# A fused attention and token-mixing kernel: a new order of all steps on every engine, other piece widths for the first filler products, and one store moved

## The chip, the cores and the metric

The kernel runs on one core of one Trainium2 chip. The metric is the time of one execution on the device, in microseconds (us); lower is better. A core has five engines that each work through a queue of their own in order: TensorE (PE: matrix products, with a second stream for its weight loads, PEld), VectorE (DVE), ScalarE (ACT), GpSimd (POOL) and SyncE (SP, which here only issues DMAs). Engines wait for one another by semaphores. Loads that change the type from f32 to bf16 are issued by POOL; plain stores and loads by SP, ACT or POOL.

## The reference

Two stages over 8 batches. Attention has 8 heads of 64 columns and 576 rows; the packed queries `p` have 32 rows.

```python
p_packed = sm_attn(p, k, v)            # softmax(p k^T / 8) v          (32 x 64 per head)
out      = sm_attn(q, p_packed, p_packed)   # softmax(q p_packed^T / 8) p_packed
x  = out as (batch, 576, 512)
wq, wk = x @ w_q, x @ w_k              # 512 -> 64
W_tok  = einsum('bsd,btd->bst', wq, wk) / 8
mixed  = einsum('bst,btd->bsd', W_tok, x)
result = relu(mixed) @ w_out           # 8 x 576 x 512, f32
```

## The kernel before, in words

Everything is unrolled, batch by batch, and written as steps. One string, `ORDER`, lists all 522 steps; the loop at its end (lines 604 to 625) runs through it and issues each step's instructions. The order of the string is therefore the order within each engine's queue: two steps on different engines may overlap, two on the same engine may not pass each other. A step is written `NAME.batch.part@engine=banks`: `@A` is ACT, `@V` DVE, `@P` POOL; a step without a letter is PE's, except loads (`LD`, issued by POOL unless marked) and stores (`ST`, `STF`, `STH`, issued by SP unless marked). The number after `=` names the 2 KB PSUM banks that the product is written to.

The steps of one batch, with the line where the instruction is recorded (copies are recorded in helpers: L127 on ACT, L131 on DVE, L129 on POOL; block transposes in L242):

| step | engine | what | line |
|---|---|---|---|
| LD.k, LD.v, LD.q (LD.r, LD.g: half of one) | POOL | load with f32 to bf16; v is two DMAs | L179, L176, L185 (L182, L156) |
| LD.E, LD.H | ACT, SP | first p and half of k of batch 0, as f32 | L164, L171 |
| EC, HC, EX, PB | ACT, DVE | turn these into the operands of the first products | L127, L242, L131 |
| KT, QV, PT | DVE | block transpose of k, of q, of the packed result | L242 |
| S1, X1, TE | PE, ACT, DVE | p k^T; exponential; transpose of it | L278/L288, L296/L299, L242 |
| PV, RC, PP | PE, DVE, DVE | times v; reciprocal of the sum; scaling | L321, L325, L329 |
| QK, QKE, QD | PE, ACT or DVE, any | packed result times w_k, w_q; copy; second copy | L342, L127/L131/L129 |
| S2, X2, RS, RR, AM | PE, ACT, DVE, DVE, DVE or POOL | q times packed result; exponential; row sums; reciprocal; scaling | L379, L384, L400, L405, L411 |
| AT, AE | PE, copy | transpose; copy to SBUF | L425/L420 |
| WKQ, WE, GM, GE, Y, YE | PE and copies in turn | the two 64-column products, x^T wk, and its product with the packed result | L447/L452, L473, L483, L490/L492 |
| MX, MR, RL, RLR | PE, ACT or DVE | mixing product (MR: the rest rows) and relu | L498, L504, L509/L511 |
| OT, OE (OEF, OH, OEH) | PE, copy | tiles of relu times w_out, and copies of them; OT.b.4 is the rest rows of two batches | L546/L583 |
| ST (STF, STH) | SP, POOL, ACT | 512 KB (256, 128 KB) of the output | L565, L567, L592, L596 |

`WARM.n=bank` (lines 615 to 621) multiplies zeros: n x 128 columns of f32, in pieces of at most 512 columns, whose result nobody reads. Each f32 piece leaves two records in the trace. They fill PE's queue where nothing else is ready: 27 units ahead of the first real product S1.0, 12 steps with 78 units in all, the last just ahead of batch 3. `HOLD.v7` is a tiny DMA on SP that waits for the last load of v, so that SP's stores behind it don't begin earlier. `SET` steps write constants and zeros; `SET.tab` is a tiny exponential on ACT.

There are four buffers each for k, v and q, six for the output, two or three for most others. Eight loads may be under way on POOL's queue; the next one waits for the eighth before it.

Of the kernel before, what the change touches and what calls it, by code (L numbers as in the profile page):

```python
# [11 lines left out]
ORDER = """
SET.warm@V LD.E0@A LD.H@S LD.g0 SET.mask@V LD.E1@S LD.W0 SET.v0@V EC@A LD.v0 SET.tab@A HC@A LD.q0 LD.W1
SET.pz0@V EX@V PB.0.1@V PB.0.0@V SET.idf@V SET.aff@P PB.0.3@V PB.0.2@V KT.0.1@V KT.0.0@V QV.0.1@V WARM.27=0
S1.0=0,1,2 X1.0.0@A WARM.6=3 PV.0.0=4,5 PV.0.1 RC.0@V PP.0.0@V PP.0.1@V PT.0@V WARM.6=3 QK.0=3 LD.r0 QV.0.0@V
SET.v1@P SET.v3@P WARM.1=6 S2.0.2=6,7 LD.k1 S2.0.0=0,1 LD.P2 X2.0.0@A S2.0.1=4,5 RS.0.0@V LD.P3 X2.0.1@A
X2.0.2@A SET.v2@V RS.0.2@V RR.0.2@V AM.0.2@V KT.1.2@V RS.0.1@V RR.0.1@V LD.P0 RR.0.0@V AM.0.0@V LD.v1
WARM.18=2 S1.1=0,1,2 SET.idb@V AM.0.1@V QKE.0@A QD.0@V WARM.3=4 AT.0.2=3 SET.aT0@V X1.1.0@A AT.0.0=4 AE.0.0@A
PV.1.0=6,7 LD.P1 PX@V LD.q1 LD.k2 LD.v2 AE.0.2@A PV.1.1 RC.1@V PP.1.1@V SET.aT1@V AT.0.1=5 AE.0.1@V
WKQ.0.0=0,1 WARM.2=2 WKQ.0.1 WKQ.0.2 WE.0.0@A SET.aT2@V WE.0.1@A WARM.4=2 GM.0=7 GE.0@A WARM.1=2 Y.0=2,3  # L20
QV.1.2@V PP.1.0@V PT.1@V S2.1.1=4,5 KT.2.2@V LD.q2 X2.1.1@A S2.1.0=0,1 S2.1.2=6,7 YE.0@A MX.0.0=4,5 LD.k3 LD.O
LD.v3 X2.1.2@A S1.2=2,3,6,7 RS.1.1@V RR.1.1@V AM.1.1@P X2.1.0@A RS.1.0@V RR.1.0@V X1.2.1@A X1.2.0@A TE.2.1@V
WARM.5=0 AT.1.1=0 AE.1.1@A RL.0.0@A AM.1.0@P QK.1=1 TE.2.0@V QKE.1@A QD.1@A LD.k4 PV.2.0=6,7 PV.2.1 AT.1.0=2
RS.1.2@V RR.1.2@V AM.1.2@V AT.1.2=3 AE.1.2@A AE.1.0@V WARM.2=0 WKQ.1.0=4,5 LD.q3 WKQ.1.2 WKQ.1.1 WE.1.0@A
MR.0=0,1 MX.0.1=2,3 RC.2@V WE.1.1@A GM.1=4 RLR.0@A QV.2.2@V RL.0.1@A PP.2.0@V PP.2.1@V PT.2@V KT.3.2@V QK.2=5
QKE.2@A S2.2.3=6,7 S2.2.2=0,1 GE.1@A LD.v4 X2.2.3@A Y.1=2,3 YE.1@V X2.2.2@A WARM.3=5 MX.1.1=4,5 MR.1=6,7
# [11 lines left out]
LD.q7 S1.6=0,1,4,5 ST.0.0@P OE.2.0@A PT.5@V AE.4.3@V WKQ.4.0=6,7 QV.5.2@V WKQ.4.1 X1.6.1@A X1.6.0@A TE.6.0@V
WKQ.4.2 OT.3.0=2,3 OT.3.1 WE.4.2@A MR.3=4,5 RLR.3@A TE.6.1@V S2.5.2=0,1 S2.5.3=6,7 OE.3.0@V X2.5.3@A X2.5.2@A
HA.5@P GM.4=4 OT.3.4=5 OEF.3.4@A ST.2.1 GE.4@V Y.4=2,3 YE.4@A PV.6.0=6,7 PV.6.1 RC.6@V ST.1.4 QV.6.2@V  # L40
PP.6.1@V QK.5=4 QKE.5@A MX.4.0=0,1 ST.2.0 RL.4.0@A PP.6.0@V PT.6@V RS.5.4@V RR.5.4@V AM.5.3@P QD.5@A
MX.4.1=2,3 RL.4.1@A OT.3.2=4,5 KT.7.2@V OT.3.3 S2.6.2=0,1 X2.6.2@A OE.3.1@A S2.6.3=6,7 X2.6.3@A MR.4=2,3
RLR.4@V RS.6.4@V OT.4.0=0,1 OT.4.1 OE.4.0@A AM.5.2@P QK.6=4 S1.7=6,7,2,3 X1.7.1@A AT.5.3=5 OT.4.2=0,1 AT.5.2=2
QKE.6@A ST.3.1 X1.7.0@A AE.5.3@V WKQ.5.0=4,5 QD.6@V WKQ.5.1 AE.5.2@A WKQ.5.2 RR.6.4@V AM.6.3@V OT.4.3 TE.7.1@V
AT.6.3=3 TE.7.0@V AE.6.3@V AM.6.2@P WE.5.2@A GM.5=6 PV.7.0=4,5 PV.7.1 OE.4.1@A QV.7.0@V GE.5@A Y.5=0,1 RC.7@V
PP.7.1@V PP.7.0@V AT.6.2=7 WKQ.6.0=2,3 WKQ.6.1 QV.7.1@V AE.6.2@A WKQ.6.2 PT.7@V YE.5@A MR.5=6,7 MX.5.0=0,1
RL.5.0@V ST.1.0 RLR.5@A WE.6.2@A MX.5.1=4,5 OT.5.4=6 RL.5.1@A GM.6=7 GE.6@A S2.7.2=2,3 X2.7.2@A S2.7.1=0,1
S2.7.0=4,5 OEF.5.4@V RS.7.2@V QK.7=7 ST.0.1@P ST.4.1@P ST.3.4@P QKE.7@V Y.6=2,3 RR.7.2@V AM.7.2@P OT.5.0=6,7
X2.7.1@A ST.3.0 X2.7.0@A YE.6@A MX.6.1=0,1 RS.7.0@V MR.6=4,5 RLR.6@A RR.7.0@V AM.7.0@P RS.7.1@V MX.6.0=2,3
OT.5.1 RL.6.1@A OT.5.2=4,5 OE.5.0@A RR.7.1@V AM.7.1@V ST.5.4 AT.7.0=0 ST.1.1 AT.7.1=1 RL.6.0@A AT.7.2=6 ST.4.0  # L50
ST.5.0 QD.7@V OT.5.3 AE.7.2@A OE.5.1@A AE.7.0@V WKQ.7.0=2,3 WKQ.7.2 AE.7.1@V WKQ.7.1 OT.6.0=0,1 WE.7.0@V
WE.7.1@A GM.7=7 GE.7@A OT.6.1 ST.5.1 OE.6.0@V Y.7=4,5 YE.7@A OT.6.2=2,3 MX.7.0=6,7 MX.7.1=4,5 OEF.6.2@V
# [7 lines left out]
def kernel(  # L60
# [542 lines left out]

    with tc.manual_schedule():
        for item in ORDER.split():
            name, _, bk = item.partition("=")
            name, _, eng = name.partition("@")
            f = name.split(".")
            if f[0] == "LD":
                load(f[1], eng)  # L610
            elif f[0] in ("HOLD", "TOUCH"):
                hold(f[1])
            elif f[0] == "SET":
                setup(f[1], eng)
            elif f[0] == "WARM":
                n = 128 * int(f[1])
                while n > 0:
                    w = min(n, 512)
# [1 line left out]
                    nc.tensor.matmul(bank(int(bk), [w]), warm[:, 0:P], rhs, start=True, stop=True)  # L620
# [33 lines left out]
```

## Time and profile before

| | us |
|---|---|
| median of 3 runs | 106.24 (105.89 to 106.82) |
| the profiled execution | 105.26 |
| its span, first to last instruction | 103.5 |
| busy: PE / DVE / ACT / POOL | 93.6 / 76.4 / 65.9 / 47.3 |
| products on zeros (L620), busy | 21.4, all before 37.5 |
| OT products (L546), busy | 29.5 and 3.6 |
| first real product / last product ends | 9.57 / 99.0 |

The times of instructions come from the profiled execution, so that a sum over them is made against 105.26 us: 103.5 of span and 1.8 around it. The page has the busy tenths of each engine in 40 slices of 2.6 us, the chain of work that ended last, groups of instructions by line, and the DMA queues. The timeline gives start and duration of each instruction (or of neighbouring equal ones, with x and their number), and in brackets how long the engine was idle before it and what ended that. The tensor clock was granted at 1.0 throughout.

### The profile page before, as it was taken

To read this page: it belongs to the slowest core of one execution; us is meant where nothing else is said; L and a number is where in the kernel's file an instruction comes from. 1 tells how busy PE (TensorE), PEld (TensorE's weight loads), DVE (VectorE), ACT (ScalarE), POOL (GpSimd) and SP (SyncE) were. 2 spreads that over 40 slices of the span, in tenths; PEclk is the share of its full clock that TensorE was granted. 3 is DMA by queue.
4 is the path that set the end of the run, shared out by engine and by line. 5 is a ranking of instruction groups with operands and counts; after the bars stand their busy time and mean duration, and the time that the engine had idled before them with its cause. 6 is when DMAs were issued, how large, how long until landed. Compare 5 with 4: busy or idle time off the path is not lost.

```text
span 103.5 us, 3532 instructions
## 1 busy us (share of the span) xinstructions
PE 93.6 (90%) x1502; PEld 54.5 (53%) x1518; DVE 76.4 (74%) x152; ACT 65.9 (64%) x116; POOL 47.3 (46%) x67
## 2 busy tenths in 40 slices
PE   5997999999799899978999999999999899999920
...
DVE  5146265999898889598797979749999988549510
ACT  0190406063588986578999879889987798936220
...
PEclk9999999999999999999999999999999999999999
DMA  2999999999999999999999999999999999995794
GB/s 87 245 176 205 198 206 201 208 213 208 209 212 213 205 208 212 213 208 212 212 209 209 212 210 206 219 208 204 212 284 403 408 412 416 398 421 221 284 379 161
DMA packets 14015, 25.16 MB, mean 243 GB/s; under 512 B 2160, under 2 KB 7024, under 8 KB 14000
## 3 DMA queue, kind: packets, MB, share of 16 engines
...
q8 instruction: 12, 0.20, 0.7%
q10 hardware_dynamic: 416, 0.20, 0.7%
...
HBM read 30.28 MB, written 9.44 MB: 384 GB/s over the span
## 4 chain that ended last, share of the span: by engine, by line
PE 59%; DMA 15%; DVE 8%; ACT 6%; POOL 5%; issue 2%; SPq 0%; ACTq 0%; POOLq 0%; DVEq 0%
PE ps L546 23%; DMA k_sb<-in_k_dram 12%; PE ps L620 9%; PE ps L321 4%; PE ps L379 4%; POOL a L411 4%; DMA o<-in_p_dram 3%; PE ps L452 3%; PE ps L425 3%; DVE kT L242 3%; PE ps L278 2%; PE ps L473 2%; DVE rs L400 2%; PE ps L498 2%; PE ps L447 2%
## 5 line engine op out<-in xcount | busy, mean ns | idle before, releaser
L546 PE MATMUL ps<-wout,relu 128*128 128x512 bf16 x111 | 29.5, 380 | 1.4 <-ACT wkq L127 0.6
L620 PE MATMUL ps<-o 128*128 128x512 f32 (+3 forms) x50 | 21.4, 555 | 1.2 <-DVE o L134 1.2
L411 POOL TENSOR_TENSOR a<-e,rr 128x256 bf16<-128x256 f32 (+2 forms) x12 | 14.9, 1247 | 16.5 <-ACT e L384 8.7
L546 PEld LDWEIGHTS <-relu 128*128 128x128 bf16 x124 | 10.8, 98 | 12.6 <-issue 2.1
L127 ACT ACTIVATE o<-ps 128x1024 f32<-128x1024 f32 (+2 forms) x14 | 12.7, 917 | 3.6 <-DMA out_dram<-o 2.0
L384 ACT ACTIVATE e<-ps 128x256 f32<-128x256 f32 (+2 forms) x19 | 11.1, 629 | 5.5 <-PE ps L379 5.5
L620 PEld LDWEIGHTS ps<-o 128*128 128x128 f32 x50 | 9.2, 203 | 9.2 <-issue 7.2
L242 DVE STREAM_TRANSPOSE qT<-q_sb 128x1152 uint32<-128x1152 uint32 (+1 forms) x10 | 11.2, 1121 | 3.1 <-DMA q_sb<-in_q_dram 3.1
L400 DVE TENSOR_REDUCE rs<-e 128x16 f32<-128x512 f32 (+2 forms) x13 | 11.1, 855 | 3.1 <-ACT e L384 2.9
L509 ACT ACTIVATE relu<-ps 128x1024 bf16<-128x1024 f32 (+1 forms) x12 | 11.7, 988 | 0.7 <-PE ps L498 0.7
L176 POOL DMA_DIRECT2D v_sb<-in_v_dram x16 | 10.1, 632 | 4.4 <-DMA q_sb<-in_q_dram 1.7
L242 DVE STREAM_TRANSPOSE kT<-k_sb 128x1152 uint32<-128x1152 uint32 (+1 forms) x9 | 11.0, 1228 | 0.5 <-DMA k_sb<-in_k_dram 0.4
L127 ACT ACTIVATE wkq<-ps 128x448 bf16<-128x448 f32 (+1 forms) x10 | 7.1, 731 | 3.2 <-PE ps L447 2.1
L131 DVE COPY o<-ps 128x512 f32<-128x512 f32 (+2 forms) x6 | 4.9, 824 | 3.8 <-PE ps L546 1.7
L299 ACT ACTIVATE e1T<-ps 128x576 bf16<-128x576 f32 x12 | 7.4, 656 | 0.3 <-PE ps L288 0.2
L321 PE MATMUL ps<-v_sb,e 64*64 64x192 bf16 x288 | 7.5, 245 | 0.1
L179 POOL DMA_DIRECT2D k_sb<-in_k_dram x7 | 5.1, 730 | 5.0 <-DMA k_sb<-in_k_dram 3.2
L452 PE MATMUL ps<-aT,pqk 128*128 128x256 bf16 (+1 forms) x48 | 6.7, 247 | 0.3 <-POOL pqk L129 0.3
L321 PEld LDWEIGHTS <-e 64*64 64x64 bf16 x288 | 5.8, 107 | 1.8 <-DVE e L242 0.6
L296 ACT ACTIVATE e<-ps 128x1152 bf16<-128x1152 f32 x2 | 2.3, 1130 | 7.0 <-PE ps L278 7.0
L379 PE MATMUL ps<-ppT,qT 64*128 64x64 bf16 x320 | 6.3, 190 | 0.0
L185 POOL DMA_DIRECT2D q_sb<-in_q_dram x6 | 4.3, 723 | 4.2 <-DMA q_sb<-in_q_dram 2.5
...
## 6 DMA issues: line engine op xcount, KB each, us to landing
...
q_sb<-in_q_dram POOLq DMA_DIRECT2D x6, 576.0 KB, 13.8
...
```

What stands on the lines that cost most here:

```text
L127: nc.scalar.activation(o, i, COPY)
L176: nc.gpsimd.dma_start(v_bufs[b % NL][halves(i), 0:7:2], src)
L242: nc.vector.transpose(o, i)
L321: nc.tensor.matmul(T["pv", b][halves(cc), i], lhsT, rhs, start=n == 0, stop=n == R - 1, skip_group_check=True)
L379: nc.tensor.matmul(ps[:, y, t - t0, i], lhsT, rhs, start=e == 0, stop=e == 1)
L384: nc.scalar.activation(e2[:, t0:t1].rearrange("a t (i y n) -> a y (t i) n", i=2, y=2), T["s2", b, c].rearrange("a y t i n -> a y (t i) n") ...
L400: nc.vector.tensor_reduce(rs[:, t0 * H:t1 * H], src, axis=AX, op=ADD)
L411: e.tensor_tensor(a2[:, t0:t1].rearrange("a t i (u l) -> a (t i u) l", l=L), e2v(b, c), T["rr", b][:, t0 * H:t1 * H].to_broadcast((P, (t1 ...
L452: nc.tensor.matmul(o, pqk[:, i, Dl:], aT[:, i, c0:c1], start=i == 0, stop=i == 1)
L509: nc.scalar.activation(o, i, RELU)
L546: nc.tensor.matmul(ps, lhsT, wout[:, j, :], start=j == 0, stop=j == NJ - 1)
L620: nc.tensor.matmul(bank(int(bk), [w]), warm[:, 0:P], rhs, start=True, stop=True)
```

## The change

All 522 steps stay, with the same instructions, except that steps move in the order and some change engine; the number of `WARM` steps goes from 12 to 14 and their units from 78 to 85. Before S1.0 there are 23 units in place of 27, in pieces of at most 192 columns in place of 512; between S1.0 and the last of them 62 units in place of 51.

- Head: on DVE, `SET.v3`, `SET.pz0` come ahead of `SET.warm`; `SET.tab` comes ahead of `EC` on ACT; POOL's first load is `LD.P3`, then `LD.g0`; the memsets of `SET.v0` and `SET.mask` and `PB.0.0` move from DVE to POOL; `KT.0.0` runs ahead of `KT.0.1`.
- Loads: the four small parts of p and the two small weights change places among batch 0's and 1's loads; q5 goes ahead of k6; k5, k6, k7 come later in POOL's queue, behind scaling steps (AM).
- From ACT to DVE: QKE.2, QKE.4, GE.1 to 3, RLR.1, 2, 5 to 7, OE.0.0, AE.2.2, AE.7.2, RL.3.1, RL.5.1, RL.6.0, WE.4.2, OEF.3.4, OEF.6.3, OEF.7.4, YE.4, YE.7.
- From DVE to ACT: QD.0, QD.7, AE.0.1, AE.4.3, YE.1, RL.1.0, RL.1.1, RL.5.0, OE.3.0, OE.6.0, OEF.6.2, OEF.7.0, OEF.7.2, GE.4, RLR.4, RLF.7.0.0, RLF.7.0.1.
- POOL gets QD.3, QD.5 (from ACT), QD.6, AM.6.3, AM.7.1 (from DVE) and gives SET.v3, AM.1.0, QD.4 to DVE.
- Stores: POOL issues ST.1.1, ST.2.0, ST.2.1, ST.0.1 in place of ST.0.0, ST.0.1, ST.4.1, ST.3.4; SP issues `ST.6.0` (tiles 0 and 1 of batch 6) ahead of `STF.6.2` in place of behind it.

The diff, cut to the parts of the order that the prediction speaks of, and the changed loop:

```diff
-SET.warm@V LD.E0@A LD.H@S LD.g0 SET.mask@V LD.E1@S LD.W0 SET.v0@V EC@A LD.v0 SET.tab@A HC@A LD.q0 LD.W1
-SET.pz0@V EX@V PB.0.1@V PB.0.0@V SET.idf@V SET.aff@P PB.0.3@V PB.0.2@V KT.0.1@V KT.0.0@V QV.0.1@V WARM.27=0
...
-RLR.1@A S1.3=2,3,0,1 X1.3.0@A RS.2.4@V RR.2.4@V AM.2.2@V RL.1.1@V OT.1.4=6 OEF.1.4@A OT.0.0=2,3 OT.0.1 LD.q4
-X1.3.1@A TE.3.0@V OE.0.0@A AT.2.2=7 AE.2.2@A OT.0.2=0,1 TE.3.1@V PV.3.0=4,5 PV.3.1 LD.k5 AM.2.3@P AT.2.3=6
-AE.2.3@A RC.3@V PP.3.1@V PP.3.0@V PT.3@V KT.4.2@V OT.0.3 LD.v5 LD.k6 QD.2@P MX.1.0=2,3 WKQ.2.0=4,5 WKQ.2.2
...
-QD.4@P LD.q6 WE.3.2@A S1.5=6,7,0,1 X1.5.1@A RR.4.4@V AM.4.3@P OT.2.2=2,3 GM.3=4 OT.2.3 X1.5.0@A TE.5.1@V
-TE.5.0@V GE.3@A Y.3=0,1 YE.3@V AM.4.2@P LD.k7 PV.5.0=6,7 PV.5.1 OE.2.1@A RC.5@V PP.5.1@V MX.3.0=4,5 LD.v7
...
+SET.v3@V SET.pz0@V LD.E0@A SET.warm@V SET.tab@A SET.aT1@V LD.H@S LD.P3 LD.E1@S EC@A EX@V PB.0.1@V LD.g0
+SET.v0@P HC@A PB.0.3@V PB.0.2@V KT.0.0@V KT.0.1@V LD.v0 PB.0.0@P WARM.23.192=0 S1.0=0,1,2 X1.0.0@A WARM.6=3
...
+KT.3.2@V WE.1.1@A GM.1=7 QK.2=6 GE.1@V WARM.3=0 Y.1=0,1 X2.2.2@A QKE.2@V S1.3=2,3,6,7 X2.2.3@A RS.2.4@V
+RR.2.4@V LD.v4 X1.3.1@A TE.3.1@V X1.3.0@A TE.3.0@V OT.0.0=4,5 OT.0.1 LD.q4 YE.1@A AM.2.2@V OT.0.2=6,7 OE.0.0@V
+OT.0.3 MR.1=2,3 OE.0.1@A RLR.1@V MX.1.1=0,1 PV.3.0=4,5 PV.3.1 RL.1.1@A RC.3@V PP.3.1@V PP.3.0@V KT.4.2@V
+AM.2.3@P QD.2@P AT.2.3=2 AE.2.3@A OT.1.4=3 MX.1.0=6,7 AT.2.2=5 OEF.1.4@A AE.2.2@V WKQ.2.0=0,1 PT.3@V QV.3.2@V
+WKQ.2.1 RL.1.0@A WKQ.2.2 WE.2.2@A S1.4=2,3,4,5 X1.4.1@A X1.4.0@A TE.4.1@V OT.1.0=6,7 LD.k5 GM.2=0 QK.3=1
...
+S2.4.2=2,3 X2.4.2@A LD.k6 KT.5.2@V S2.4.3=4,5 OT.2.2=0,1 X2.4.3@A QD.4@V RS.4.4@V RR.4.4@V AM.3.2@P AT.3.2=6
+WKQ.3.0=2,3 WKQ.3.1 AE.3.2@A LD.v6 WKQ.3.2 WE.3.2@A S1.5=4,5,6,7 OT.2.3 X1.5.1@A TE.5.1@V GM.3=2 GE.3@V
+OT.2.0=6,7 LD.q6 X1.5.0@A Y.3=4,5 TE.5.0@V PV.5.0=2,3 PV.5.1 OE.2.1@A YE.3@V MX.3.0=0,1 AM.4.2@P RC.5@V
+PP.5.0@V AM.4.3@P PP.5.1@V RL.3.0@A MX.3.1=4,5 RL.3.1@V LD.k7 QV.5.2@V OT.2.1 OE.2.0@A LD.v7 AT.4.2=2 AE.4.2@A
...
+OE.3.1@A ST.3.1 OT.4.1 OE.4.0@A QK.6=6 QKE.6@A S1.7=2,3,0,1 RS.6.4@V AM.5.3@P AT.5.3=7 OT.4.2=4,5 AM.5.2@P
+QD.5@P RR.6.4@V X1.7.1@A ST.3.4 X1.7.0@A AE.5.3@V TE.7.0@V AT.5.2=6 AE.5.2@A AM.6.3@P QD.6@P TE.7.1@V ST.2.0@P
+WKQ.5.0=0,1 WKQ.5.1 WKQ.5.2 WE.5.2@A OT.4.3 OE.4.1@A ST.4.1 AT.6.3=7 QV.7.1@V AE.6.3@V GM.5=2 PV.7.0=0,1
...
                 n = 128 * int(f[1])
+                wide = int(f[2]) if len(f) > 2 else 512
                 while n > 0:
-                    w = min(n, 512)
+                    w = min(n, wide)
```

More of the change, by code (lines that the diff above doesn't have):

```diff
@@ L18 @@
[L18 to L26, printed above, removed]
-RLR.1@A S1.3=2,3,0,1 X1.3.0@A RS.2.4@V RR.2.4@V AM.2.2@V RL.1.1@V OT.1.4=6 OEF.1.4@A OT.0.0=2,3 OT.0.1 LD.q4
@@ L38 @@
[L38 to L52, printed above, removed]
@@ L53 @@
-STF.6.2 MR.7=0,1 RLR.7@A RLF.7.1.1@A OT.6.3 RLF.7.0.1@V ST.6.0 OEF.6.3@A STF.6.3 OT.7.4=2 OEF.7.4@A ST.7.4
-RLF.7.0.0@V RLF.7.1.0@V OT.7.0=0 OEF.7.0@V STF.7.0 OT.7.2=1 OEF.7.2@V STF.7.2 OT.7.1=7 OEF.7.1@A STF.7.1
-OH.7.0=5 OEH.7.0@A STH.7.0 OH.7.1=6 OEH.7.1@V STH.7.1@A
+SET.v3@V SET.pz0@V LD.E0@A SET.warm@V SET.tab@A SET.aT1@V LD.H@S LD.P3 LD.E1@S EC@A EX@V PB.0.1@V LD.g0
+SET.v0@P HC@A PB.0.3@V PB.0.2@V KT.0.0@V KT.0.1@V LD.v0 PB.0.0@P WARM.23.192=0 S1.0=0,1,2 X1.0.0@A WARM.6=3
+PV.0.0=4,5 PV.0.1 RC.0@V LD.q0 SET.mask@P SET.idf@V SET.aT0@V QV.0.1@V PP.0.0@V LD.P2 LD.r0 PP.0.1@V PT.0@V
@@ new lines @@
+SET.v2@V LD.W0 QV.0.0@V WARM.15=3 S2.0.2=6,7 LD.k1 LD.W1 SET.aT2@V LD.P1 KT.1.2@V S2.0.1=0,1 X2.0.1@A RS.0.1@V
+SET.v1@P S2.0.0=2,3 X2.0.0@A LD.v1 LD.P0 WARM.8=4 QK.0=4 RR.0.1@V AM.0.1@V QKE.0@A LD.q1 RS.0.0@V SET.aff@P
+SET.idb@V WARM.3=5 S1.1=0,1,2 X1.1.0@A WARM.6=5 PV.1.0=4,5 PV.1.1 X2.0.2@A RR.0.0@V AT.0.1=3 AM.0.0@V AT.0.0=2
+AE.0.0@A RC.1@V PP.1.1@V RS.0.2@V RR.0.2@V AM.0.2@V AE.0.1@A QD.0@A WARM.5=0 WKQ.0.0=0,1 AT.0.2=5 LD.k2
+AE.0.2@A WARM.1=6 WKQ.0.2 LD.v2 WE.0.0@A WKQ.0.1 LD.q2 LD.k3 WE.0.1@A WARM.3=6 GM.0=5 PP.1.0@V PT.1@V QK.1=4
```

32 lines of the change are left out of this document (23 added, 9 removed).

## The prediction

> **What bounds the kernel now.** I read the page's slices first, then the busy time by stage, then the chain of waits and the timeline around the places where the order changes. The slices:
>
> ```profile
> PE   5997999999799899978999999999999899999920
> DVE  5146265999898889598797979749999988549510
> ACT  0190406063588986578999879889987798936220
> DMA  2999999999999999999999999999999999995794
> PEclk9999999999999999999999999999999999999999
> ```
>
> PE is nearly always busy and the DMA engines are busy throughout, at full tensor clock. They bound different stages. Until about 45 us PE waits for loads and the zero products fill the gaps; from there to 99 us PE has real work in its queue all the time. Busy time by stage (length, PE, PEld, DVE, ACT, POOL, ...):
>
> ```profile
> 31.00:38.00 7.00, 6.71 (x176) 4.28 (x172) 5.79 (x13) 6.29 (x14) 3.85 (x6) 1.00 1.17 207
> 45.00:52.00 7.00, 6.11 (x154) 3.88 (x157) 5.85 (x8) 5.72 (x10) 1.97 (x4) 1.00 1.15 211
> 52.00:59.00 7.00, 6.52 (x133) 4.18 (x134) 6.29 (x11) 6.70 (x13) 3.48 (x4) 1.00 1.16 211
> 59.00:66.00 7.00, 6.89 (x118) 3.82 (x119) 5.59 (x11) 5.85 (x10) 6.10 (x8) 1.00 1.15 209
> 66.00:73.00 7.00, 6.89 (x164) 4.07 (x165) 5.36 (x12) 5.97 (x12) 1.61 (x2) 1.00 1.14 211
> ```
>
> PE idles 0.89 us in 45 to 52, 0.48 in 52 to 59 and 0.11 in each stage after: 2.7 us from 38 us to its last product. That is about all a better order can win there. Behind the last product at 99.0 come the copy (0.42), the store's landing (3.0) and the end, 4.5 us that the change leaves as they are. So the question is: when does PE get through batch 3's and 4's gates, and does it starve afterwards? Two instructions set the gates (timeline):
>
> ```profile
> 35.56 1.38 DVE L242 STREAM_TRANSPOSE kT<-k_sb 128x1152 uint32<-128x1152 uint32 x1 [0.42 <-DMA k_sb<-in_k_dram]
> 43.98 1.34 DVE L242 STREAM_TRANSPOSE kT<-k_sb 128x1152 uint32<-128x1152 uint32 x1
> ```
>
> The first is KT.3, which had to wait for its load; the second is KT.4, 0.25 us behind the landing of k4, which the chain of waits puts at 43.73. The bytes ahead of both in the load queue are the same after the change, and the queue moves 205 to 213 GB/s whatever is done beside it, so I take these two landings as fixed (within 0.3 us).
>
> **The change, part by part.**
>
> *Head.* EC waited for its load until 4.88, then for a table load that SET.tab now brings on before it:
>
> ```profile
> 4.88 1.28 ACT L127 ACT_TABLE_LOAD   x1 [4.88 <-DMA o<-in_p_dram]
> 8.07 1.44 DVE L242 STREAM_TRANSPOSE kT<-k_sb 128x576 uint32<-128x576 uint32 x2
> 9.57 1.25 PE L278 MATMUL ps<-o,kT 128*64 128x128 bf16 x36 [0.69 <-DVE kT L242]
> ```
>
> EC, EX, three PB and HC then end near 6.45 and KT.0.0 near 7.2. KT.0.1 needs g0: it was issued at 1.27 and landed 6.3 us later; behind LD.P3 (0.53 to issue) it lands at 8.1 or a little later. S1.0 could start at 8.95, 0.6 earlier than now. But it is queued behind the zero products, which start at 2.2 (SET.v3 0.54, SET.pz0 0.48, SET.warm 0.27 from 0.87) in place of 1.2. They are 16 pieces with two passes each. How long is a pass of 192 columns? The chain of waits has the neighbours, two passes each:
>
> ```profile
> 15.01 0.42 PE ps L620 x2
> 24.23 0.43 PE ps L620 x2
> ```
>
> The first is a piece of 128 columns, the second one of 256: 0.21 per pass both times. The wider follows its columns; the narrower follows its f32 weight load (0.19). For 192 the bounds are 0.16 (by columns) and 0.21 (by load); I take 0.21, the value on either side. Before the clock is up everything takes twice that: weight loads start 0.86 apart until 3.92 and 0.43 apart from 4.63 on, 3.4 us after the first product. So 3.4 us hold 8 passes, the other 24 take 5.0, and S1.0 starts at 10.6 (by columns: 9.0).
>
> [...]
>
> *Front, to batch 3.* Between S1.0 and the last zero product there are 11 more units, at 0.213 each 2.3 us. They cost nothing while PE would have waited anyway. Now S1.3 starts at 37.69, with MX.1.1 and MR.1 (0.4) ahead of it that the new order puts behind: 37.3 on equal terms. In the new order KT.3 ends at 36.94, then GE.1 on DVE (0.29) and Y.1 (0.2) must pass: 37.45. Counted by PE instead: from S1.0 on the real products ahead of S1.3 need 13.8 us at their spacings (S1 1.25 twice, PV 0.87 three times, WKQ 0.95 twice, S2 0.7 three times and the small ones) and 62 units 13.2; now they lose 3.1 to waits and restarts. With S1.0 at 10.6 and a loss of 1 us, S1.3 starts at 38.6; with S1.0 at 9.0, KT.3 decides: 37.5.
>
> *Batch 3 to 4.* Between S1.3 and S1.4 PE does the same work plus those 0.4. S1.4 began at 45.86, and can't begin before KT.4 ends at about 45.3. QD.2 on POOL no longer sits behind a load that waits for k4, which cost 0.30 of PE. Against that, RL.1.0 (1.02) goes to ACT ahead of WE.2.2. In the new order ACT runs OE.0.1, RL.1.1, AE.2.3 (to about 44.9), then WKQ.2 takes 0.95: S1.4 at 45.9. With S1.3 a good half us late I put +0.2 to this whole front, bounds -0.5 (KT.4's end) and +1.1 (S1.3 at 38.7, the slack of 0.3 used up).
>
> *Batch 3 to 7.* Moves from ACT to DVE between S1.4 and S1.7 (GE.2, RLR.2, QKE.4, GE.3, RL.3.1, WE.4.2, OEF.3.4, YE.4, and QD.4 from POOL) add 5.1 us to DVE; moves away (AE.4.3, OE.3.0, GE.4, RLR.4) take 2.6. DVE was busy 23.1 of the 28 us from 45 to 73; it becomes 25.6, 91%. WE on DVE for 896 columns has no row: 0.92 on ACT and twice the 0.62 of its 448 columns on DVE bound it; I take 1.2. I followed each engine's queue from S1.4 on with the durations of the rows. Three places come out late:
>
> - S1.5 to PV.5. QD.4, RS.4.4 and RR.4.4 stand ahead of TE.5.1, GE.3 and TE.5.0 on DVE:
>
> ```profile
> 56.90 1.49 DVE L400 TENSOR_REDUCE rs<-e 128x40 f32<-128x1280 f32 x1
> 58.81 0.77 DVE L242 STREAM_TRANSPOSE e<-e1T 128x288 uint32<-128x288 uint32 x2
> 59.64 0.94 PE L321 MATMUL ps<-v_sb,e 64*64 64x192 bf16 x36
> ```
>
>   KT.5 ends at 57.8, QD.4 58.0, RS.4.4 59.5, RR.4.4 59.9, then 0.45 + 0.29 + 0.45: TE.5.0 at 61.1. PE has OT.2.3, GM.3 and OT.2.0 until 60.3 and waits there for Y.3 (GE.3) and PV.5: 0.6.
> - Batch 4: RL.3.1 (1.2) behind batch 5's scalings delays OT.3.0 by 0.2, and WE.4.2 behind KT.6 and PT.5 delays GM.4: together 0.3.
> - Batch 5 and 6: RS.6.4 (1.49) and RR.6.4 (0.4) stand ahead of AE.5.3, and AE.5.2 behind X1.7.1 and X1.7.0 on ACT. WKQ.5 waits 0.5 and its third part 0.2 more; 0.1 of it was idle now. So 0.6.
>
> The loads k5, k6, k7 come some 3 to 4 us later in POOL's queue, behind scalings of 1.9 to 2.1 us. Eight DMAs under way are 8 to 12 us of bytes, so the DMA engines don't run dry, and I cost it at nothing; with that cover gone each us would be a us on KT.6 or KT.7.
>
> *Tail.* S2.7.0 goes first and the scalings of batch 7 all run on POOL (0.6 + 1.05 in place of 0.75 on DVE for the last); PE has 4 us of products in between, so nothing waits. SP's and POOL's stores change places; the output buffers come free earlier for batch 7, and ST.0.1, now issued near 87 in place of 78.8, lands by 93 to 95 (three POOL stores took 9.1 in the median), just before OEF.6.2 needs the room. ST.6.0 ahead of STF.6.2 costs nothing, since OE.6.0 is done first. PE's waits between 80 and 87 were 0.33 and partly go: -0.3, bounds -0.6 and +0.6 (ST.0.1 late).
>
> Sum: +0.2 + 0.6 + 0.3 + 0.6 - 0.3 = **+1.4 us**. The profiled execution would go from 105.26 to 106.7; the median of the runs, 0.98 above it, from 106.24 to **107.6**.
>
> **The rivals.**
>
> - *The zero products delay the front.* S1.0 at 10.6 and the 11 units at full price put S1.3 at 38.7 and S1.4 0.9 later than in my sum: 108.5. For it: the two rows at 0.21. Against: KT.3's load hides up to 1.5 us of it.
> - *Everything is gated where it was.* The front as now (0.0) and the three late places cost 0.2 together, because ACT, with 1.6 us less to do, feeds DVE earlier than I reckon: 106.4. This also stands for a change that does nothing.
> - *Faster: PE's idle time goes.* The waits from 38 us on (2.7 us) and the load at QD.2 are what a new order is able to remove. With S1.4 at 45.4 (-0.5) and of the 2.2 us behind it half gone: -1.6, 104.6. It decides at PV.5: if TE.5.0 ends before OT.2.0 does (60.3), DVE isn't the late engine and this rival holds. DVE at 91% speaks against it.
>
> **How the numbers follow.** Chances: forecast 0.32, delayed front 0.20, gated as before 0.24, faster 0.24. About 1% (1.06 us) is what a measurement of this kernel can tell from no change. Slower by more: 0.52; within: 0.24; faster: 0.24. The range runs from the faster rival's 104.6 to 109.0, the delayed front with ST.0.1 late in addition (108.5 + 0.5); the forecast's own is 107.0 to 108.2.
>
> **What would show it.** In the new profile: the table load before 4 us; the zero passes 0.21 apart and S1.0 at 10.6 (or 9.0); S1.3 between 37.5 and 38.7; S1.4 near 46; waits of PE products for DVE's e transposes near PV.5, and of WKQ.5 for its aT copy; DVE near 9 tenths from 52 to 78; the last product 1.4 us later, at 100.4. I am wrong if DVE's queue order lets TE.5 and AE.5.3 through in time, or if the load queue runs dry behind the later k5 to k7.

## The result, and the profile after

The changed kernel takes 107.01 us in the median of 22 runs (105.94 to 108.30), the kernel before 105.97 beside it (22 runs, 105.05 to 107.31). The ratio is 1.0091, with a 95% interval of 1.0067 to 1.0116: **slower by 0.9%**, a little under the 1% that I had named as the bound of "no change", though the interval does not reach down to 1. The ratio leaves out the runs that took over 1.5% longer than their kernel's fastest, seven of these 22 and two of before's; the two medians alone would give 1.0098.

The two profiles must be read with care. After's profiled execution took 107.88 us, 0.87 above its median; before's took 105.26, now 0.71 below its. So of the 2.62 us between the two profiles, 1.58 belong to these two executions and 1.04 to the kernels. The slices of the profile after:

```profile
PE   1999999999999999899998999999999999999950
...
DVE  5072069934998989978599988997996999526410
ACT  5140401344688785379978787988898696659440
...
PEclk9999999999999999999999999999999999999996
DMA  3989999999999999999999999999999999984874
```

PE is now busy from the second slice on, with hardly a digit below 9: the waits that before's slices showed near 9, 27, 35 and from 44 to 49 us are filled. Yet the kernel is slower. A busy PE proves little here: the 32 passes on zeros ahead of S1.0 count as busy like any product. The stages (length, then busy time of PE, PEld, DVE, ACT and POOL with counts, clock, DMA share, GB/s):

```profile
31.00:38.00 7.00, 6.98 (x138) 4.03 (x138) 6.56 (x17) 5.76 (x13) 2.99 (x4) 1.00 1.17 209
45.00:52.00 7.00, 6.79 (x167) 4.48 (x167) 5.24 (x12) 6.10 (x11) 1.83 (x3) 1.00 1.15 209
52.00:59.00 7.00, 6.70 (x116) 3.64 (x115) 6.33 (x12) 5.80 (x7) 3.91 (x5) 1.00 1.16 211
59.00:66.00 7.00, 7.00 (x130) 4.17 (x129) 6.23 (x13) 5.37 (x8) 5.66 (x8) 1.00 1.14 206
66.00:73.00 7.00, 6.90 (x166) 4.28 (x165) 6.02 (x11) 6.01 (x12) 2.86 (x5) 1.00 1.13 210
```

From 45 us on PE idles 0.21, 0.30, 0.00 and 0.10 us of 7 where before's rows had 0.89, 0.48, 0.11 and 0.11. How much of that is real is a question for the end of the section on the prediction. DVE does carry more there: 5.24 + 6.33 + 6.23 + 6.02 = 23.8 against 23.1 before. I had forecast 25.6.

Where is the time, then? Starts of the batches' first products, from the two timelines:

| | before | after | difference |
|---|---|---|---|
| S1.0 | 9.57 | 10.57 | +1.00 |
| S1.1 | 20.17 | 21.32 | +1.15 |
| S1.2 | 28.86 | 31.09 | +2.23 |
| S1.3 | 37.69 | 40.07 | +2.38 |
| S1.4 | 45.86 | 48.77 | +2.91 |
| last product ends | 99.03 | 101.93 | +2.90 |
| end of the span | 103.5 | 105.8 | +2.3 |

From S1.4 to the last product both kernels take the same: 53.17 and 53.16 us. All of the loss lies ahead of S1.4. MX.1.1 and MR.1 (0.4) were ahead of S1.3 and are now behind it. On equal terms the pieces are +1.00 up to S1.0, +1.78 from S1.0 to S1.3 (29.50 against 28.12 - 0.4), +0.13 from S1.3 to S1.4 (8.70 against 8.17 + 0.4), nothing behind it, and -0.6 in the tail behind the last product (3.9 against 4.5). They add up to 2.3.

S1.0, which I had forecast as late, shows in this timeline of PE, with the last of its operands, KT.0.1 on DVE, between:

```profile
2.35 8.29 PE L621 MATMUL ps<-o 128*128 128x192 f32 x32 [2.35 <-DVE o L134]
7.93 0.78 DVE L242 STREAM_TRANSPOSE kT<-k_sb 128x576 uint32<-128x576 uint32 x1 [0.52 <-DMA k_sb<-in_k_dram]
10.57 0.60 PE L278 MATMUL ps<-o,kT 128*64 128x128 bf16 x14
```

The operand is there at 8.71. S1.0 starts at 10.57, right behind the 32 passes on zeros, which alone hold it for 1.86 us. Further on:

```profile
40.07 0.48 PE L288 MATMUL ps<-kT,pT 32*32 32x288 bf16 x32
...
45.21 0.94 PE L321 MATMUL ps<-v_sb,e 64*64 64x192 bf16 x36 [0.71 <-DVE o L131]
...
48.77 0.48 PE L288 MATMUL ps<-kT,pT 32*32 32x288 bf16 x32
```

The middle line is PV.3. It waits 0.71 us for a copy on DVE (L131), which I had not seen coming.

### The profile page after: what moved, and what is told of

It reads as the page before. It is cut to its first block, busy times and chain, and to the rows that moved or that the text cites. A ratio compares the mean times of both kernels' runs of the same rounds, so it can differ in the third digit from the quotient of the medians.

```text
span 105.8 us, 3599 instructions
## 1 busy us (share of the span) xinstructions
PE 98.1 (93%) x1542; PEld 60.7 (57%) x1542; DVE 75.4 (71%) x150; ACT 66.2 (63%) x109; POOL 49.8 (47%) x76
## 4 chain that ended last, share of the span: by engine, by line
PE 80%; DVE 9%; ACT 5%; POOL 2%; issue 1%; DVEq 0%; POOLq 0%; ACTq 0%
PE ps L546 24%; PE ps L621 20%; PE ps L321 6%; PE ps L379 5%; PE ps L452 4%; PE ps L425 3%; PE ps L498 3%; DVE rs L400 3%; ACT e L384 3%; PE ps L447 3%; PE ps L278 2%; PE ps L473 2%; PE ps L288 2%; PE ps L342 2%; POOL a L411 2%; DVE a L411 2%
## 5 line engine op out<-in xcount | busy, mean ns | idle before, releaser
L546 PE MATMUL ps<-wout,relu 128*128 128x512 bf16 x124 | 30.5, 380 | 0.0
L621 PE MATMUL ps<-o 128*128 128x192 f32 (+5 forms) x74 | 24.9, 478 | 2.5 <-DVE o L134 2.3
L411 POOL TENSOR_TENSOR a<-e,rr 128x1024 bf16<-128x1024 f32 (+2 forms) x13 | 15.6, 1212 | 22.5 <-DVE rr L405 14.2
L127 ACT ACTIVATE o<-ps 128x1024 f32<-128x1024 f32 (+2 forms) x17 | 15.0, 888 | 6.9 <-PE ps L546 6.3
L621 PEld LDWEIGHTS ps<-o 128*128 128x128 f32 x74 | 15.1, 227 | 7.3 <-issue 3.8
L509 ACT ACTIVATE relu<-ps 128x1024 bf16<-128x1024 f32 (+1 forms) x14 | 12.7, 933 | 2.2 <-PE ps L498 1.1
L325 DVE RECIPROCAL rec<-ps 128x2 f32<-128x2 f32 x8 | 1.3, 157 | 10.2 <-PE ps L321 10.2
L127 ACT ACTIVATE aT<-ps 128x128 bf16<-128x128 f32 (+2 forms) x11 | 5.3, 506 | 3.6 <-PE ps L425 2.1
L127 ACT ACTIVATE wkq<-ps 128x448 bf16<-128x448 f32 (+1 forms) x9 | 6.3, 713 | 1.7 <-PE ps L452 1.4
L379 PEld LDWEIGHTS <-qT 64*128 64x128 bf16 x320 | 5.5, 94 | 2.3 <-issue 0.7
```

What stands on the lines that cost most here:

```text
L127: nc.scalar.activation(o, i, COPY)
L379: nc.tensor.matmul(ps[:, y, t - t0, i], lhsT, rhs, start=e == 0, stop=e == 1)
L411: e.tensor_tensor(a2[:, t0:t1].rearrange("a t i (u l) -> a (t i u) l", l=L), e2v(b, c), T["rr", b][:, t0 * H:t1 * H].to_broadcast((P, (t1 ...
L509: nc.scalar.activation(o, i, RELU)
L546: nc.tensor.matmul(ps, lhsT, wout[:, j, :], start=j == 0, stop=j == NJ - 1)
```

## The experiments

Most kernels are joins of the two orders, or the order after with one step put back. All of them compute the whole output; those with fewer or other products on zeros change only work whose result nobody reads.

**1. Which half costs?** The order before up to S1.4 and the order after from there on, and the other way round:

```diff
 h1: (order before) ... WKQ.2.1 OE.0.1@A WE.2.2@A
+QV.3.2@V RL.1.0@A S1.4=2,3,4,5 X1.4.1@A ... (order after)
 h2: (order after) ... RL.1.0@A WKQ.2.2 WE.2.2@A
+LD.k5 LD.v5 LD.k6 S1.4=6,7,0,1 X1.4.0@A ... (order before)
```

> The order of before up to S1.4 of batch 4 (its 78 units of zero products too), behind it the order and the engines of after. FRONT theory (the changed kernel loses its time ahead of S1.4, because the zero products hold PE's queue): no difference from before, ratio 0.997 to 1.003, S1.4 at about 45.9. BODY theory (as forecast: DVE's longer queue behind S1.4 costs 1.2 us): ratio 1.008 to 1.014, S1.4 at 45.9 and the last product 1.2 us later than before's 99.0. LOADS theory (the load queue runs dry at 5 to 8 us, so that every gate is late): as FRONT, since the head is before's.

> The order of after up to S1.4 (its 85 units of zero products too), behind it the order and the engines of before. FRONT and LOADS: the whole loss is here, ratio 1.007 to 1.013, S1.4 at 47 to 48.8, from there to the last product the 53.2 us of before. BODY: ratio 1.000 to 1.004.

Measured: h1 1.0406 (1.0346 to 1.0466), h2 1.0165 (1.0124 to 1.0206). Neither fits a theory, because each join brought waits that neither kernel has. In h1:

```profile
48.45 0.48 PE L288 MATMUL ps<-kT,pT 32*32 32x288 bf16 x32 [1.92 <-ACT relu L509]
48.86 1.89 PE L546 MATMUL ps<-wout,relu 128*128 128x512 bf16 x4
```

S1.4 waits 1.92 us for RL.1.0, whose bank it needs. Behind this wait four products of OT take 1.89 us in place of 1.03: the trace's record of the clock has it at half from 48.90 us on, for 3.41 us. There is a second pause of 1.80 us at 73.4 (more on it below), and again 3.41 us at half, from 76.20. (h1's runs go from 109.36 to 112.94 us; this one took 112.42.) h2 lost 0.9 us in two waits at its S1.4. These two kernels decide nothing on the halves.

**2. The join again, with the banks in line.** In the part behind the join all banks were renumbered so that S1.4 finds its banks free; h1b's front also has 18 units of zeros and 28 tiny products (32 columns, bf16) in place of 27 units, which makes the number of PE's instructions that of after.

```diff
 h1b: (order before up to S1.4)
-WARM.27=0
+WARM.18=0 TINY.28=0
+...  S1.4=6,7,0,1 X1.4.1@A X1.4.0@A TE.4.1@V OT.1.0=2,3 ... (after, banks renumbered)
 h2b: (order after up to S1.4)
+...  S1.4=2,3,4,5 X1.4.0@A OT.1.0=0,1 GM.2=6 ... (before, banks renumbered)
```

> The order of before up to S1.4 and that of after behind it again, without two things that spoiled the first such kernel: the PSUM banks of the second part are exchanged in pairs so that S1.4 no longer waits for RL.1.0, and 28 tiny bf16 products on zeros replace 9 units of zeros ahead of S1.0, so that every later product stands near the place in PE's instruction stream that it has in after. FRONT theory (the loss of after lies ahead of S1.4, the part behind it costs the same in both): S1.4 at 45.9 to 46.5, 53.2 us from there to the last product, ratio 0.996 to 1.006. BODY theory: 54.4 us from S1.4 to the last product, ratio 1.008 to 1.016. CODE theory (PE pauses in mid-group where a fetch of its instructions, a 16 KB packet of the instruction queue, is not done in time, and which group that is depends on the count of instructions ahead): no pause at QK.5, where the first kernel of this kind had one of 1.80 us.

> The order of after up to S1.4 and that of before behind it, with the PSUM banks of the second part exchanged in pairs so that S1.4 doesn't wait for copies of WKQ.2 and MX.1.0, as it did for 0.9 us in the first such kernel. FRONT: S1.4 at 47 to 48.8 and 53.2 us from there to the last product; ratio 1.006 to 1.012, as after. BODY: from S1.4 52 us or less to what after has, ratio 1.000 to 1.004.

Measured: h1b 1.0169 (1.0110 to 1.0228), h2b 1.0102 (1.0065 to 1.0138). h2b is as slow as after (1.0091), with the new body gone: **the front alone carries the loss**. From S1.4 it needs 53.34 us to the last product, as the old body does in before (53.17) and the new one in after (53.16). Its profiled execution (107.24 us) lies at its median, unlike after's and before's. In it S1.0 starts at 9.76, only 0.19 behind before's, and yet S1.3 (39.50) and S1.4 (48.20) come 1.81 and 2.34 later than there. So S1.0's start with this head differs between executions (10.48 in h2, 10.52 in e10), and a late S1.0 isn't the whole loss. h1b still has a wait of its own making (ACT and PE):

```profile
46.81 1.02 ACT L509 ACTIVATE relu<-ps 128x1024 bf16<-128x1024 f32 x1
...
47.89 1.04 PE L546 MATMUL ps<-wout,relu 128*128 128x512 bf16 x4 [1.50 <-ACT relu L509]
```

RL.1.0 stands behind WE.2.2 on ACT and OT.1.0 waits 1.50 us for it. Its total therefore says little about the body; from S1.5 on it takes 41.48 us, after 41.82, and before 41.26 (42.12 less OT.2.2, 0.86, which stands on the other side). The bodies are even within 0.6, and the three late places, 1.2 us in my forecast, don't show. What the new body would be worth under the old front without a join's wait stays open.

**3. The width of the first zeros.** One number is taken back:

```diff
-WARM.23.192=0
+WARM.23=0
```

> after with one edit: the first 23 units of zeros in pieces of 512 columns again. All theories: the products on zeros end near 9.0 and S1.0 starts at 9.0 to 9.1 in place of 10.57. FRONT: some of these 1.5 us reach S1.4, as far as no load gates it: ratio to before 1.000 to 1.006, that is 0.4 to 1.0 us faster than after. LOADS: k3 and k4 land as late as in after, S1.3 and S1.4 move by 0.3 us at most, ratio 1.006 to 1.010. BODY: the same ratio as after, 1.007 to 1.011.

Measured: 1.0217 (1.0178 to 1.0257), slower still, although S1.0 starts at 9.11 and S1.4 at 47.31, both 1.46 us earlier than in after's profile. The width isn't what moved S1.0: the next kernel has the same first zeros, and its S1.0 came at 10.37, because PE ran at half rate for 5.9 us there and for 3.4 us here (how this is read stands in 6). The gain was lost again in the middle of one step, QK.5, eight small products:

```profile
70.27 0.27 PE L342 MATMUL ps<-wqk,ppT 64*64 64x128 bf16 x3
71.95 0.32 PE L342 MATMUL ps<-wqk,ppT 64*64 64x128 bf16 x5 [1.41 <-issue]
```

PE stands still for 1.41 us in the middle of a group, and the profile names nothing that it waits for ("issue"). In the records of the DMA engines a 16 KB transfer of instructions began at 69.62 (the page counts 12 of the kind, with some 250 of PE's products and weight loads from one to the next on average, so I take them for PE's), and PE went on 2.3 us later. In h1 it was 72.82 and 75.25, again in QK.5.

**4. Wide pieces and 11 units fewer** (WARM steps taken out between S1.1 and S1.3):

```diff
-WARM.23.192=0 ... WARM.1=6 ... WARM.1=6 ... WARM.7=0 ... WARM.2=7 ... WARM.2=7 ... WARM.3=0
+WARM.23=0     ...                           WARM.5=0
```

> after with two edits: the first 23 units in pieces of 512 columns, and 11 units fewer between S1.1 and S1.3 (the last two steps of 1, two of 2 and one of 3 units taken out, the one of 7 cut to 5), so that 51 are left behind S1.0 as in before. FRONT: S1.3 comes 2 us or more earlier than after's 40.1, at 37.5 to 38, and the ratio to before is 0.990 to 1.001. LOADS: S1.3 waits for KT.3 at 38.7 and the ratio stays at 1.004 to 1.008. BODY: 1.005 to 1.010.

Measured: 1.0194 (1.0155 to 1.0233). From S1.1 to S1.3 it takes 18.00 in place of 18.75 us: 11 units, 2.35 us at full price, bring 0.75. The gain goes to a pause of 1.23 us that ends at 73.99, this time in an OT step (instruction transfer at 71.73), and PV.3 waits 1.1 us for its bank.

**5. Is the pause in e1 a matter of where the instructions stand?** Narrow passes are many instructions: 32 in after's front, 12 in e1's. e7 has e1's wide pieces, fewer of them, and 26 tiny products that bring PE's count back to after's 1542.

```diff
-WARM.23.192=0
+WARM.11=0 TINY.26=0
```

> after with the first zero products changed: 11 units in pieces of 512 columns and 26 tiny bf16 products of 32 columns in place of 23 units in pieces of 192; PE's later instructions keep the places in the stream that they have in after, which they lost with the wide pieces alone. CODE: the pause of 1.41 us at QK.5 is gone, from S1.4 to the last product 53.2 us as in after, and the time is 1.0 to 1.8 us below that of the wide pieces alone: ratio to before 1.003 to 1.011. If the place in the stream has nothing to do with it, the pause stays and the ratio is 1.018 to 1.026.

Measured: 1.0000 (0.9968 to 1.0032), 105.91 us; its profiled execution took 107.57, 1.66 above that, so only its order of things is read. The same place in QK.5:

```profile
71.33 0.44 PE L342 MATMUL ps<-wqk,ppT 64*64 64x128 bf16 x8
71.70 0.60 PE L498 MATMUL ps<-wkq,y 64*128 64x512 bf16 x4
```

Eight products run through in one piece; the pause is gone, and with it and the shorter zeros 2.2% against e1. So the pause seems to hang on what stands ahead in PE's stream, not on QK.5 as such; h1b, with 28 tiny products, has none either. That the late instruction transfer causes it fits three kernels with pauses (1.41, 1.80, 1.23 us) but wasn't tested by itself. The number of instructions alone doesn't decide: before has 1518 weight loads, as many as h1, the same 12 transfers, and no pause.

**6. When the zeros start.** One memset first on DVE, as it was before:

```diff
-SET.v3@V SET.pz0@V LD.E0@A SET.warm@V SET.tab@A
+SET.warm@V SET.v3@V SET.pz0@V LD.E0@A SET.tab@A
```

> after with one step moved: SET.warm is DVE's first instruction again, so that PE's zero products start at 1.2 in place of 2.35; nothing else on PE changes. FRONT: S1.0 starts at 8.9 to 9.4 in place of 10.57 (the half-rate stretch of PE ends earlier), S1.4 1 to 1.6 us earlier than in after's profile, ratio to before 0.998 to 1.006. LOADS: S1.4 moves by 0.3 us at most and the ratio stays at 1.007 to 1.011. BODY: the same.

Measured: 1.0024 (0.9990 to 1.0058), 106.06 us: 0.7% of the 0.9% is back.

```profile
1.20 7.40 PE L621 MATMUL ps<-o 128*128 128x192 f32 x32 [1.20 <-DVE o L134]
8.53 1.23 PE L278 MATMUL ps<-o,kT 128*64 128x128 bf16 x36
```

The first product on zeros starts at 1.20 in place of 2.35, and S1.0 at 8.53 in place of 10.57. That is 2.04 us for 1.15: the passes also sped up sooner. That second part needn't come from the edit: h2b has after's head, and its passes sped up 4.4 us behind the first, much like e8's. The stages of 1 us with the number of passes in each show it, for after:

```profile
3.30:4.30 1.00, 1.00 (x5) 1.00 1.15 271
...
5.30:6.30 1.00, 1.00 (x4) 1.00 0.98 145
...
7.30:8.30 1.00, 1.00 (x5) 1.00 1.07 177
8.30:9.30 1.00, 1.00 (x7) 1.00 1.17 175
9.30:10.30 1.00, 1.00 (x8) 1.00 1.15 196
```

and for e8:

```profile
3.30:4.30 1.00, 1.00 (x5) 1.00 1.19 248
4.30:5.30 1.00, 1.00 (x5) 1.00 0.94 123
5.30:6.30 1.00, 1.00 (x7) 1.00 1.07 153
6.30:7.30 1.00, 1.00 (x9) 1.00 0.90 143
```

Columns are length, PE busy with the number of passes, clock, DMA share and GB/s. At half rate the passes start 0.32 apart, four or five counted in a us; at full rate 0.16, seven to nine. After's passes become fast between 8 and 8.5 us, about 6.1 us behind the first; e8's between 5 and 5.6, 4.3 behind the first. The column of the granted clock says 1.00 throughout, so it can't be read there, only from the spacing. The trace's own record of the clock agrees with the spacing: it begins at 8.45 us in after and at 5.48 in e8, at full clock, and has nothing ahead of that.

**7. OE.0.0 back on ACT:**

```diff
-OT.0.0=4,5 OT.0.1 LD.q4 YE.1@A AM.2.2@V OT.0.2=6,7 OE.0.0@V
+OT.0.0=4,5 OT.0.1 LD.q4 YE.1@A AM.2.2@V OT.0.2=6,7 OE.0.0@A
```

> after with one step on another engine: OE.0.0 (the copy of batch 0's first two output tiles, 1.2 us) on ACT as in before. PV.3 is written to the banks that this copy empties, and in after waited 0.71 us for it behind AM.2.2 on DVE. If that wait is a part of the loss, PV.3 starts 0.5 to 0.9 us earlier relative to S1.3, S1.4 0.4 to 0.7, and the ratio to before is 1.002 to 1.007. If KT.4 or ACT's own queue is late anyway, the ratio stays at 1.007 to 1.012.

Measured: 1.0017 (0.9978 to 1.0055), 106.03 us, although S1.0 starts at 10.52 as in after.

```profile
40.01 0.48 PE L288 MATMUL ps<-kT,pT 32*32 32x288 bf16 x32
...
44.37 0.94 PE L321 MATMUL ps<-v_sb,e 64*64 64x192 bf16 x36
...
48.01 0.48 PE L288 MATMUL ps<-kT,pT 32*32 32x288 bf16 x32
```

PV.3 no longer waits. It starts 4.36 us after S1.3 (5.14 in after), and S1.4 8.00 after S1.3 (8.70). What held it in after shows in after's timeline of DVE:

```profile
42.29 1.73 DVE L411 TENSOR_TENSOR a<-e,rr 128x256 bf16<-128x256 f32 x1
43.94 1.21 DVE L131 COPY o<-ps 128x1024 f32<-128x1024 f32 x1
45.08 0.41 DVE L511 TENSOR_SCALAR rem<-ps 128x256 bf16<-128x256 f32 x1
46.22 0.17 DVE L325 RECIPROCAL rec<-ps 128x2 f32<-128x2 f32 x1 [0.74 <-PE ps L321]
46.43 0.61 DVE L329 SCALAR_TENSOR_TENSOR pp<-ps,rec,mask 128x128 bf16<-128x128 f32 x2
46.95 1.37 DVE L242 STREAM_TRANSPOSE kT<-k_sb 128x1152 uint32<-128x1152 uint32 x1
```

AM.2.2 (1.73) and then OE.0.0 (1.21) until 45.15: OE.0.0 empties the bank of OT.0.0, which PV.3 needs (both are `=4,5`). Behind them RC.3, PP.3 and KT.4 are late too. KT.4 ran at 46.95, though k4 had landed at 44.34; it ends at 48.32, before S1.4 starts, so what reached S1.4 is PV.3's delay on PE itself.

AM.2.2 is itself part of it. The same instruction took 0.42 us in before. What differs is POOL's scaling AM.2.3 beside it (two lines of before, then one of after):

```profile
39.52 0.42 DVE L411 TENSOR_TENSOR a<-e,rr 128x256 bf16<-128x256 f32 x1
39.64 2.07 POOL L411 TENSOR_TENSOR a<-e,rr 128x1024 bf16<-128x1024 f32 x1 [0.54 <-DMA v_sb<-in_v_dram]
...
41.83 1.90 POOL L411 TENSOR_TENSOR a<-e,rr 128x1024 bf16<-128x1024 f32 x1 [4.44 <-DVE rr L405]
```

In before, AM.2.2 starts first. In after two transposes (TE.3) stand ahead of it on DVE, POOL starts 0.46 us earlier, and AM.2.2 ends at 44.02, 0.29 behind POOL's end at 43.73. All eleven kernels with after's front show 1.73 us, the three with before's 0.42. With 0.42, OE.0.0 would be done some 1.3 us sooner by these rows, more than the 0.71 that PV.3 waits; that is an estimate, since no kernel here puts AM.2.2 back ahead of the transposes.

**8. Both undone:**

```diff
-SET.v3@V SET.pz0@V LD.E0@A SET.warm@V ... OE.0.0@V
+SET.warm@V SET.v3@V SET.pz0@V LD.E0@A ... OE.0.0@A
```

> after with the two edits that each brought it to the time of before: SET.warm first on DVE, OE.0.0 on ACT. FRONT: the two gains lie in different places (S1.0; PV.3) and add up: S1.4 at 46 to 46.5 in a profile, 53.2 us from there to the last product, ratio to before 0.992 to 0.999, faster than both kernels. If the load of k4 (landed at 43.7 to 44.4, KT.4 behind it) gates S1.4 by then, only part is left: 0.998 to 1.003.

Measured: 0.9968 (0.9946 to 0.9990), 105.57 us. Each edit alone had won 0.7% against after, both together win 1.2%: they nearly add up. What is left of the change is then **no slower than the kernel before**: 0.3% faster here, with an interval that just leaves out 1, which those of its two variants below (0.9994 and 0.9981) do not. S1.0 8.94, S1.3 38.56, S1.4 46.71, last product at 99.73.

**9. Is it the loads?** In after POOL waits 1.11 us for EX ahead of PB.0.0 and issues q0 at 6.23 (4.1 before); k3 lands at 36.40 (35.54 before). On top of e11, three early steps go back from POOL to DVE:

```diff
-SET.v0@P HC@A ... PB.0.0@P ... SET.mask@P
+SET.v0@V SET.mask@V ... HC@A PB.0.3@V PB.0.2@V PB.0.0@V
```

> The same two edits, and POOL's first steps as in before: the memsets of SET.v0 and SET.mask and PB.0.0 on DVE again, so that POOL issues its loads without the 1.1 us for which it waited for EX. LOADS: 5 to 8 us the queue moves 175 GB/s or more in place of 134, k3 lands 0.5 us or more earlier and S1.4 too: ratio 0.004 or more below that of the two edits alone. FRONT: PE's queue decides as far as S1.3, the ratio is within 0.003 of it.

Measured: 0.9994 (0.9970 to 1.0018), 106.04 us. The load of q0 goes out at 4.5 in place of 6.1 and k3 lands at 36.01 in place of 36.35, but the time isn't better than e11's. Its S1.0 started 0.51 later than e11's, by a longer stretch at half rate; from S1.0 to S1.4 it takes 37.50 against 37.77. By these two executions earlier loads are worth 0.3 us at the most; only 0.34 of k3's 0.86 us were undone.

**10. Fewer zeros on top of e11** (11 units out, as in 4, each of the five steps taken out replaced by two tiny products):

```diff
-WARM.1=6 ... WARM.1=6 ... WARM.7=0 ... WARM.2=7 ... WARM.2=7 ... WARM.3=0
+TINY.2=6 ... TINY.2=6 ... WARM.5=0 ... TINY.2=7 ... TINY.2=7 ... TINY.2=0
```

> The same two edits, and 11 units of zeros between S1.1 and S1.3 fewer, each taken product replaced by two tiny bf16 products so that the later instructions keep their places in PE's stream. If the zero products only fill waits: S1.3 at most 0.8 us earlier (that is what their removal brought in the kernel with wide pieces), ratio within 0.004 of the two edits alone. If they hold up PE's queue at full price: S1.3 1.5 us or more earlier, ratio 0.006 or more lower, unless KT.3 or KT.4 gates.

Measured: 0.9981 (0.9949 to 1.0014), 105.87 us. S1.1 to S1.3 takes 18.00 in place of 18.87 us, so 0.87 of the 2.35 us. In this execution S1.0 starts at 9.45 in place of 8.94 (a longer stretch at half rate again), which takes 0.5 back, and 0.23 is left at S1.4. The time isn't better than e11's. The 11 further units look worth some tenths at most.

## Why the prediction was right and wrong

**The sum.** 107.6 was forecast, 107.01 measured, by the ratio +0.96 us in place of +1.4. The sign and about the size are right, but the terms aren't: I had +0.2 ahead of S1.4 and +1.2 behind it in the three late places; measured is the whole loss ahead of S1.4 and nothing behind it up to the last product. That the total came near is luck. The part of the loss that e8 takes back belongs to the rival of the zeros that delay the front, which I had given 0.20; the part that e10 takes back, OE.0.0 on DVE, was in neither the sum nor a rival. The rival's marks were S1.0 at 10.6 and S1.3 at 38.7, on which S1.4 depends; measured 10.57 and 40.07 in a profile that is 0.87 above its median, and 9.76 and 39.50 in h2b's.

**S1.0 at 10.6**: right for this execution, by two errors that cancel. I took 0.21 for a pass of 192 columns, and measured is 0.16: in a row of many, the passes go by the columns (0.21 for 256 in h1b, 0.43 for 512 in before), which was the bound that I had put at 9.0. The pair of 128 columns that led me to 0.21 stood alone between other work. And I took 3.4 us at half rate, as before's trace had it; after's had about 6.1. The half-rate stretch behind the first product was 3.4 us in three profiles (before, h1, e1), then 4.3 (e8), 4.4 (h2b), 5.2 (e11), 5.8 (h1b), and about 6 in seven others (after 6.1). The sum has the one length that before's trace shows; what sets it, no run shows. With 3.4 us, S1.0 would have stood near 9.35 (2.35, 3.4 for ten passes, 22 at 0.163). The length of this stretch may have a part in the spread of the runs (2.4 us over after's 22, 2.3 over before's); one profile of each kernel can't show that.

**"They cost nothing while PE would have waited anyway", and KT.3's load as cover**: this is the step that failed. I let S1.0's delay be swallowed by the wait for KT.3. In after, e1, e8, e10 and e12, which have after's front with all its zeros, S1.0 to S1.1 takes 10.8 us, S1.1 to S1.2 9.8 to 9.9 and S1.2 to S1.3 8.9 to 9.0: the front moves as one piece, S1.3 follows Y.1 without a gap, and S1.0's start goes through to it. In the median of its runs e8's earlier zeros are worth 0.7%. The next gate does show in e7: S1.0 came at 8.03, PE then waited 0.6 us for v and 0.8 for a small weight, and S1.1 started at 20.71. In h2b too PE waited for that weight (0.17 us), which landed between 17.96 (e8) and 19.52 (h2b). So how much of an earlier start passes through depends on this load, and a start ahead of e8's 8.5 may not. I had 27.0 us of PE's work from S1.0 to S1.3 and a loss of 1 us; it is 29.5, a loss of 2.5. Of before's own 28.12 some 0.6 is that execution: the same order in h1 and h1b takes 28.72 and 28.70. Of the 1.78 us on equal terms this and the units below leave 0.3 to 0.4 open.

**The 11 further units**: between nothing and their full 2.3 us I chose nothing, with the full price in the rival. They hold S1.3 up by 0.8 to 0.9 (e3, e13), and by e13's time there is nothing of it left at the end.

**Batch 3 to 4, +0.2**: the size is right (+0.13), the working isn't. I looked at ACT (RL.1.0) and not at what OE.0.0 does on DVE behind AM.2.2, nor at the bank that PV.3 shares with it: 0.7 us, shown by e10. Without it this stretch is 0.57 us shorter than before on equal terms (8.00 against 8.57), more than the 0.30 at QD.2 that I had counted. The move of OE.0.0 was known; my sum of the moves to DVE only began at S1.4, and DVE's queue was not followed from AM.2.2 to PV.3. Nor did I ask what AM.2.2 costs beside a scaling on POOL that has already begun.

**The loads fixed within 0.3 us**: wrong by size (k3 +0.86, k4 +0.61), and, as far as e12 shows, without weight.

**The three late places, +1.2**: wrong. At PV.5, where I had put 0.6:

```profile
59.74 1.46 DVE L400 TENSOR_REDUCE rs<-e 128x40 f32<-128x1280 f32 x1
...
62.28 0.46 DVE L242 STREAM_TRANSPOSE e<-e1T 128x288 uint32<-128x288 uint32 x1
...
62.68 0.25 PE L483 MATMUL ps<-pp,g 64*64 64x128 bf16 x4
...
62.80 0.94 PE L321 MATMUL ps<-v_sb,e 64*64 64x192 bf16 x36
62.98 0.42 DVE L492 TENSOR_SCALAR y<-ps 128x256 bf16<-128x256 f32 x1 [0.24 <-PE ps L483]
```

RS.4.4 starts at 59.74, almost where I had put its end in a kernel whose S1.5 came 3 us earlier: the row sums come 0.37 us ahead of S1.5 (60.11) instead of behind it. TE.5.0 ends at 62.74, and PV.5 starts at 62.80 behind Y.3, 2.69 us after S1.5. Before it was 2.73 (59.64 less 56.91) with the same products in between, so nothing is lost here. WKQ.5 and OT.3.0 show no wait. DVE was 91% busy from 52 to 78 us (23.54 of 26), as I had expected, and yet PE idles only 0.40 us in this time: the sign that I had named for being wrong, TE.5 and AE.5.3 getting through in time, came true. The walk through the queues carried each engine's lateness forward from S1.4 and let nothing catch up; the rival "gated where it was" had named a possible reason, that ACT has less to do and feeds DVE sooner; no run tests it by itself.

**WE.4.2 on DVE**: 1.09, estimated 1.2. **Tail, -0.3**: from the last product to the end it takes 3.9 in place of 4.5, but so it does in h2b with before's order of stores (3.9), so this isn't the stores; ST.0.1, issued at 87.97, holds nobody up, which takes the upper end of my range away.

**The faster rival, and the 2.7 us of idle PE.** It decided at PV.5 by TE.5.0 ahead of OT.2.0 (62.74 against 62.75, a tie), and PV.5 went through; still nothing was won behind S1.4. What I had read as idle was in good part holes in the records (and before's rows from 38 us on add up to 2.5, not 2.7). The busy lines of e8 and e11, which have the same body:

```profile
PE 97.2 (94%) x1542; PEld 59.9 (58%) x1542; DVE 75.5 (73%) x150; ACT 66.2 (64%) x109; POOL 49.9 (48%) x76
```

```profile
PE 96.1 (93%) x1528; PEld 60.1 (58%) x1542; DVE 74.4 (72%) x149; ACT 67.2 (65%) x110; POOL 49.9 (48%) x76
```

Each product has one weight load. e8 has 1542 of both; e11 lacks 14 records of products, all of OT, and before 16 of 1518. From S1.4 to the last product e8 takes 52.96 us with 0.30 idle and e11 53.02 with 1.78: the same work and time, so that about 1.5 us of e11's idle are missing records. Before's rows, with 2.04 idle behind S1.4, must be read the same way. After has no record missing. Behind S1.4 there was hardly anything for a better order to win.
